# The opening of an attention and gated FFN kernel: crossed loads of values, another order of loads, and another order of all instructions up to the first split of h

## Chip, core and metric

The kernel runs on one core of a Trainium2 chip. The metric is the time of one execution on the device in microseconds (us). The kernel before takes 872.77 us, the median of three runs (871.47, 872.77, 873.49).

## What is computed

Attention over chunks of 64 positions, and a gated FFN over its result:

```python
# q, k, v: (8 batches, 8 heads, 576, 64), drawn as normal * 0.1, q and k times about 4
nc = S // chunk                               # 9 chunks of 64
scores = D ** -0.5 * matmul(q_c, k_c.transpose(0, 1, 2, 4, 3))
scores = scores - max(scores, axis=-1, keepdims=True)
attn = exp(scores)
attn = attn / (sum(attn, axis=-1, keepdims=True) + 1e-9)
x = matmul(attn, v_c)                         # to (4608 tokens, 512)
g = x @ w_gate                                # 512 -> 1536
h = g / (1 + exp(-g)) * (x @ w_val)
out = h @ w_out                               # 1536 -> 512
```

Inputs and outputs are float32.

## The kernel before

The 4608 tokens go in nine blocks of 512 (`N`), the 1536 inner columns in twelve parts of 128. A block's attention gives x turned, 512 features by 512 tokens, in four pieces of 128 features, one for each pair of heads. To keep precision, every factor of a product is split into an upper part in fp32r and a lower part, the rest; a product of a part (`Product`, `some`, L492) is three matmuls of 128x512 for each of the four pieces: upper by upper, upper by lower, lower by upper. For each part f a gate product (g) and a value product (v) are made, h = silu(g)\*v, h is split again, and `project` (L556 to L558) adds its products with w_out to the block's output. The weights come as 64-bit words and are joined to float32 by four steps (`scale`, `shift`, `below`, `join`, L87 to L97) and split by two more (`upper`, `lower`).

The change lies in the opening, where nothing is in memory yet and the attention of the first two blocks, a0 and a1, is done. Four head pairs make a block, two pairs make a `Couple` (class at L653). Its steps have one letter each, and they run in this order:

- S: scores of a pair (L304, 16 calls of 64x64, which the trace shows as 32 matmuls), on TensorE (PE).
- M: row maxima, on VectorE (DVE, L674). K: the maxima rounded (L678) and the rest of the rounding (L679), on DVE.
- B: two matmuls (L685) subtract the maxima from one of the couple's two banks of scores, on PE.
- E: exponentials of a bank, on ScalarE (ACT, L689). Z: their sums, DVE (L695). R: plus 1e-9 and the reciprocal, DVE (L458, L459).
- N: scores times reciprocals (L463), on DVE or on GpSimd (POOL), as L702 says: for the first couples of a0 and of a1 it is POOL.
- T: four transposes of a pair on PE (L468). C: their copy out by ACT (L708).
- X: values times probabilities of a couple (L482, 32 calls, 64 matmuls in the trace), on PE. U and L: split of the result into upper (ACT, L635) and lower part (DVE, L639).

A string (L730 to L736) is the order in which the program issues these steps, and the engines keep it, since PE, ACT and DVE are scheduled by hand. In a step such as M101 the first digit is the block, the second the pair (for S, T, C, U, L) or the couple, and the third, if any, the bank. `.8` is eight warm-up transposes of an identity (`keep_warm`, L58), whose results nobody reads. G0_12 and V0_12 are matmuls of a0's products with the first gate and value part: piece 1, third kind. Two letters are steps of weights (vs, vh, vb, vj, vu, vl: scale, shift, below, join, upper, lower of the value half of part 0; g of its gate half; w1 and w2 of parts 1 and 2). H0 is the silu of a0's first part, Q0 its product with the value. e0 and e1 are exchanges (L423): the values of a pair lie with its first head in partitions 0 to 63 and its second in 64 to 127, and X needs those of odd pairs with the halves swapped, so four ACT copies (a0) and four POOL copies (a1) of 64x512 make swapped ones (L425).

Loads are issued by SyncE (SP) in program order, L605 to L620, under a manual schedule for SP that ends with the opening. `load_v` (L420) brings the values of two pairs with one transfer of 512 KB; a pair's q and k are 512 KB, a `Half` of a weight part 512 KB, an `Up` part 1 MB.

After the string (L761 to L782) come a1's two products of part 0 (pg, pv), h1, the steps of w_out's first part (o), the split of h0 (`parts`), of w_out (`out_weights`), and `lag`, which keeps a projection back until the next one is due.

## Time and profile before

| | |
|---|---|
| runs (us) | 871.47, 872.77, 873.49; median 872.77 |
| profiled execution: span from the first to the last instruction | 870.3 us |
| runs' median less that span | 2.5 us |
| PE busy | 858.3 us, 99% of the span |
| weight loads (PEld) / DVE / ACT / POOL busy | 708.2 / 652.7 / 428.9 / 97.6 us |
| mean granted clock of PE | 0.999 |
| transfers | 217.51 MB, 250 GB/s in the mean |

The span is that of one profiled execution, which gives no other time of its own; what of a run lies around the span is read off the median. PE's busy time counts pipelined matmuls; weight loads (PEld) overlap them. A wait is written as the instruction that waited and, behind the arrow, what released it. Instructions of one line that follow each other stand in one row of the timeline.

### The profile page before, as it was taken

Reading aid. Unit: us, or ns where it says so; the run is one execution under the profiler, and the core shown is the slowest. Engines: PE = TensorE matmul, PEld = TensorE weight load, DVE = VectorE, ACT = ScalarE, POOL = GpSimd, SP = SyncE. Lnnn points to the kernel's source line nnn. Section 1 sums busy time; section 2 is a strip of 40 time slices with the busy share of each in tenths; the row PEclk is TensorE's granted clock in tenths of the full one; section 3 lists DMA queues with packets and bytes.
Section 4 is the critical chain, followed back from the end, with each engine's and each line's share of the span. In section 5 each row is a group of like instructions: output and inputs, shape, how many; then the busy total and the mean of one; then the engine's idle time right before and its main releaser. Section 6 shows DMA issues by size and latency. Waiting matters only on the chain.

```text
span 870.3 us, 14879 instructions
## 1 busy us (share of the span) xinstructions
PE 858.3 (99%) x5941; PEld 708.2 (81%) x5941; DVE 652.7 (75%) x923; ACT 428.9 (49%) x609; POOL 97.6 (11%) x86
## 2 busy tenths in 40 slices
PE   7999999999999999999999999999999999999997
...
GB/s 357 264 275 263 272 273 352 293 309 358 283 337 341 249 335 255 242 249 281 238 220 227 251 320 235 194 218 193 178 202 226 211 250 182 192 191 207 188 197 89
DMA packets 127221, 217.51 MB, mean 250 GB/s; under 512 B 57136, under 2 KB 88368, under 8 KB 117168
## 3 DMA queue, kind: packets, MB, share of 16 engines
...
## 4 chain that ended last, share of the span: by engine, by line
PE 88%; DVE 7%; DMA 2%; issue 1%; ACT 1%; SPq 0%; ACTq 0%; DVEq 0%
PE ps_a L880 24%; PE ps_gv L880 18%; PE ps_o L1229 14%; PE ps_gv L492 12%; PE ps_gv L1229 6%; PE ps_o L556 4%; PE ps_o L557 3%; PE ps_o L558 3%; PE ps_a L304 2%; PE ps_a L382 1%; DMA raw<-in_wgv 1%; DVE turned L369 1%; DMA factors<-t 1%; DVE v L884 1%; DVE rows L531 1%
## 5 line engine op out<-in xcount | busy, mean ns | idle before, releaser
L880 PE MATMUL ps_a<-x,factors 128*128 128x512 f32 x864 | 216.5, 391 | 0.5 <-DVE v L884 0.5
L880 PEld LDWEIGHTS ps_a<-x,factors 128*128 128x128 f32 x864 | 161.2, 188 | 36.8 <-DVE v L884 1.7
L880 PE MATMUL ps_gv<-x,factors 128*128 128x512 f32 x648 | 164.6, 389 | 1.0 <-DMA factors<-t 1.0
L880 PEld LDWEIGHTS ps_gv<-x,factors 128*128 128x128 f32 x648 | 121.5, 188 | 26.8 <-DMA factors<-t 1.4
L492 PE MATMUL ps_gv<-xh,w 128*128 128x512 f32 x320 | 97.9, 391 | 0.2 <-ACT xh L635 0.2
L369 DVE STREAM_TRANSPOSE turned<-s_sb 32x256 f32<-32x256 f32 x192 | 83.7, 436 | 2.7
L1229 PE MATMUL ps_o<-halves,sums 128*128 128x512 f32 (+1 forms) x324 | 72.5, 383 | 0.0
L492 PEld LDWEIGHTS ps_gv<-xh,w 128*128 128x128 f32 x320 | 59.8, 188 | 12.9 <-ACT xh L635 0.5
L1229 PEld LDWEIGHTS ps_o<-halves,sums 128*128 128x128 f32 x324 | 59.7, 188 | 12.0
L884 DVE TENSOR_TENSOR rows<-rows,ps_gv 128x512 f32<-128x512 f32 x36 | 24.7, 686 | 52.6 <-PE ps_gv L880 52.4
L531 DVE SCALAR_TENSOR_TENSOR rows<-v,rows 128x512 f32<-128x512 f32 x72 | 54.2, 752 | 12.8 <-ACT rows L1367 5.6
L1211 ACT CAST hh<-rows 128x512 fp32r<-128x512 f32 x36 | 22.4, 622 | 80.1 <-DVE rows L531 80.1
L492 PE MATMUL ps_gv<-xl,w 128*128 128x512 f32 x160 | 61.4, 393 | 0.0
L1229 PE MATMUL ps_o<-hh,left 128*128 128x512 f32 x216 | 58.4, 394 | 0.0
L556 PE MATMUL ps_o<-both,hh 128*128 128x512 f32 x144 | 56.4, 391 | 0.0
L557 PE MATMUL ps_o<-both,hh 128*128 128x512 f32 x144 | 56.0, 389 | 0.0
L558 PE MATMUL ps_o<-both,hh 128*128 128x512 f32 x144 | 56.0, 389 | 0.0
L1354 ACT ACTIVATE rows<-rows 128x512 f32<-128x512 f32 x36 | 22.8, 632 | 67.1 <-DVE rows L884 67.0
L1272 DVE TENSOR_TENSOR halves<-rows,halves 128x1024 fp32r<-128x1024 f32 x36 | 43.1, 1214 | 11.1 <-ACT halves L1268 11.1
L1229 PE MATMUL ps_gv<-halves,sums 128*128 128x512 f32 x216 | 50.4, 389 | 0.0
L1268 ACT CAST halves<-rows 128x1024 fp32r<-128x1024 f32 x36 | 37.2, 1053 | 21.4 <-DVE rows L1246 7.7
L1229 PEld LDWEIGHTS ps_gv<-halves,sums 128*128 128x128 f32 x216 | 40.5, 188 | 8.4
...
## 6 DMA issues: line engine op xcount, KB each, us to landing
...
```

The source lines that it names most:

```text
L369: nc.vector.transpose(out=self.turned[to:to + 32, p:p + 2, j, :, 32 * (i % 2):32 * (i % 2) + 32], in_=src[32 * i:32 * i + 32, :, o // 2, 3 ...
L492: nc.tensor.matmul(ps, w, x, start=first and (k, i) == which[0], stop=last and (k, i) == which[-1])
L531: nc.vector.scalar_tensor_tensor(out=h, in0=pv, scalar=2.0 ** -8, in1=h, op0=ALU.mult, op1=ALU.mult)
L556: nc.tensor.matmul(o, hl[:, ts], woh, start=f == a.steps[0], stop=False)
L557: nc.tensor.matmul(o, hh[:, ts], wol, start=False, stop=False)
L558: nc.tensor.matmul(o, hh[:, ts], woh, start=False, stop=f == a.steps[1])
L880: nc.tensor.matmul(ps, w[u][:, k], x[i][v][:, k], start=first and k == 0 and n == 0, stop=k == NK // 2 - 1 and n == 2, skip_group_check=True)
L884: nc.vector.tensor_tensor(out=t, in0=t, in1=ps, op=ALU.add)
L1229: nc.tensor.matmul(to, w[:, i, u], a[:, at], start=first and n == 0, stop=n == 2, skip_group_check=True)
L1268: nc.scalar.copy(out=t[:, 0], in_=src)
L1272: nc.vector.tensor_tensor(out=lo, in0=src, in1=hi.bitcast(F32), op=ALU.subtract)
L1354: nc.scalar.activation(h, h, AF.Silu, scale=2.0 ** -8)
```

## The change

Values of odd pairs are loaded swapped: `load_v` takes the first pair with one transfer of 128 partitions and the second with two of 64, each into the other half of the partitions, and the exchanges go. The loads stand in another order, and POOL is scheduled by hand in the opening as well. N is on POOL for both couples of a0 and the second of a1. The string is new; it now holds also a1's products (A gate, D value), the steps of w_out (o), h1 (H1), and the splits of h0 (hu, hl) and of w_out (ou, ol). The warm-ups before the loop become the string's first step.

```diff
--- before.py
+++ after.py
@@ -418,11 +418,10 @@
             return x[:, h * k:(h + 2 * y) * k].rearrange("p (i y k) -> p i y k", i=2, k=k)[:, :, 0:2 * T - 1:2]
 
         def load_v(self, p, t):
-            nc.sync.dma_start(out=t, in_=v[:, p:p + t.shape[1], self.b])
-
-        def exchange(self, t, to, copy=nc.gpsimd.tensor_copy):
+
+            nc.sync.dma_start(out=t[:, 0], in_=v[:, p, self.b])
             for h in range(2):
-                copy(out=to[h * C:(h + 1) * C], in_=t[(1 - h) * C:(2 - h) * C])
+                nc.sync.dma_start(out=t[h * C:(h + 1) * C, 1], in_=v[(1 - h) * C:(2 - h) * C, p + 1, self.b])
 
         def maxima(self, ps, m=None, tag="top"):
 
@@ -595,38 +594,31 @@
         nc.scalar.dma_start(out=waiting[f], in_=h)
 
     kept_h = []
-    loading = tc.manual_schedule(engines={mybir.EngineType.SP})
+    loading = tc.manual_schedule(engines={mybir.EngineType.SP, mybir.EngineType.Pool})
     loading.__enter__()
     a0, a1 = First(0), First(1)
     a1.places()
     a0.places()
     w, o = up[0], down[0]
-    q00 = a0.load_qk(0)
-    q01 = a0.load_qk(1)
-    wv = Half(w, 1)
-    q02 = a0.load_qk(2, 2, const, "w4")
     v0 = const.tile([P, NP, 2 * T, C], F32, name="v_t", tag="w3")
     v0 = [v0[:, p:p + 2] for p in (0, 2)]
+    q02 = a0.load_qk(2, 2, const, "w4")
+    q01 = a0.load_qk(1)
+    q00 = a0.load_qk(0)
+    q10 = a1.load_qk(0, 2, const, "w5")
+    wg = Half(w, 0)
+    q12 = a1.load_qk(2, 2, const, "w6")
+    wv = Half(w, 1)
+    a0.load_v(2, v0[1])
     a0.load_v(0, v0[0])
-    wg = Half(w, 0)
-    q10 = a1.load_qk(0, 2, const, "w5")
-    a0.load_v(2, v0[1])
-    q12 = a1.load_qk(2, 2, const, "w6")
     up[1].load()
     v1 = [ld.tile([P, 2, 2 * T, C], F32, name="v_t", tag="qk_t") for _ in range(2)]
+    a1.load_v(2, v1[1])
     a1.load_v(0, v1[0])
-    a1.load_v(2, v1[1])
     up[2].load()
     down[0].load()
     q0, q1 = [[q00, q01], [q02]], [[q10], [q12]]
-    values = []
-    for a, vs in ((a0, v0), (a1, v1)):
-        for c in range(2):
-            pool, tag = (ld, "v_t") if a is a0 else (wp, "wo")
-            odd = pool.tile([P, 2 * T, C], F32, name="v_t", tag=tag)
-            if a is a1:
-                a.exchange(vs[c][:, 1], odd)
-            values.append((vs[c][:, 0], odd))
+    values = [(t[:, 0], t[:, 1]) for t in v0 + v1]
 
     def x_of(a, p):
         return [x[:, p % 2] for x in a.x[p // 2]]
@@ -699,7 +691,7 @@
             self.a.inverse(self.z[:, :4 * T])
 
         def N(self, _):
-            self.a.scale(self.p, self.z[:, :4 * T], nc.gpsimd if (self.a.b, self.p) in ((0, 0), (1, 0)) else nc.vector)
+            self.a.scale(self.p, self.z[:, :4 * T], nc.gpsimd if (self.a.b, self.p) in ((0, 0), (0, 2), (1, 2)) else nc.vector)
 
         def T(self, q):
             self.a.turn_to(q, self.bank(1, [T, P])[q % 2])
@@ -724,29 +716,52 @@
             couples[a.b, c] = Couple(a, c, qs, values[2 * a.b + c], pools)
     products, h0 = {}, None
     steps = {"s": "scale", "b": "below", "h": "shift", "j": "join", "u": "upper", "l": "lower"}
-    weights = {"g": wg, "v": wv, "w1": up[1], "w2": up[2]}
-
+    weights = {"g": wg, "v": wv, "w1": up[1], "w2": up[2], "o": o}
+
+
+    class FirstPart:
+        def upper(self):
+            self.hh, self.hl = both_parts()
+            nc.scalar.copy(out=self.hh, in_=h0)
+
+        def lower(self):
+            nc.vector.tensor_tensor(out=self.hl, in0=h0, in1=self.hh.bitcast(F32), op=ALU.subtract)
+
+    class FirstOut:
+        def upper(self):
+            both = wp.tile([P, 2, DM], F32R, name="both", tag="wo")
+            out_now[0], self.both = both, (both[:, 0], both[:, 1])
+            nc.scalar.copy(out=self.both[0], in_=wo_raw[0])
+
+        def lower(self):
+            nc.vector.tensor_tensor(out=self.both[1], in0=wo_raw[0], in1=self.both[0].bitcast(F32), op=ALU.subtract)
+            t = store.tile([P, 2, 2, DM], F32, name="o0")
+            kept_o[0], kept_o[1], two_o[0] = t[:, 0], t[:, 1], t
+
+    first_part, first_out = FirstPart(), FirstOut()
 
     opening = """
-        S00 S01 M001 M000 vs K00 vh vb .8 B001 B000 vj E001 Z001 E000 e0 .3 S02 Z000 S03 R00 N00 M010 M011 gs
-        .10 T01 K01 gh gb C01 B011 B010 E011 T00 gj Z011 E010 Z010 R01 C00 S10 gu S11 X00 vu M101 U01 .3 V0_12
-        M100 U00 K10 G0_12 B101 e1 E101 N01 L01 B100 T02 E100 gl T03 C03 vl G0_10 S13 S12 C02 L00 M111 M110 X01
-        V0_01 w1s K11 G0_11 G0_01 U02 G0_02 U03 Z100 Z101 B111 B110 V0_21 V0_32 V0_10 w1b L02 R10 G0_22 G0_21
-        E111 V0_02 Z111 V0_22 V0_11 L03 G0_00 E110 G0_32 G0_20 G0_31 N10 V0_00 Z110 G0_30 V0_31 V0_20 V0_30 R11
-        N11 T10 T11 T13 Y0 w2s H0 w1h Q0 C10 w1j C11 T12 C12 C13 X10 U11 X11 L11 U10 U12 U13 L10 L13 w1u L12
+        .37 S03 S02 S01 M011 M010 .3 S00 K01 M001 B011 B010 M000 E011 E010 K00 .2 S10 Z011 S11 Z010 B001 M101
+        B000 E001 M100 E000 R01 gs K10 Z000 N01 .11 B100 B101 Z001 E100 S12 gb R00 S13 Z100 E101 N00 T03 M111
+        T02 C03 M110 vs Z101 C02 .6 T01 K11 T00 vb R10 B110 gh C00 B111 N10 E110 X01 E111 C01 gj T11 U03 vh
+        T10 gu X00 vj U02 gl vu G0_32 Z110 G0_22 U01 G0_21 G0_31 U00 Z111 V0_32 V0_12 C11 V0_22 vl G0_12 C10
+        V0_02 R11 G0_02 w1s V0_11 V0_01 L01 N11 X10 L00 Y0 L03 G0_10 V0_10 G0_01 L02 V0_31 G0_30 U10 T13 U11
+        T12 L10 G0_11 G0_00 C12 L11 G0_20 V0_21 C13 V0_30 w1h V0_20 H0 V0_00 X11 w1b Q0 A_12 A_01 U13 w1j A_10
+        D_02 U12 A_02 A_32 os D_12 L13 A_31 D_22 A_22 L12 A_00 w1u D_30 D_32 oh A_11 D_01 ob A_30 w1l D_31
+        A_21 A_20 D_10 D_21 H1 oj D_20 D_00 hu D_11 ou hl w2s ol
     """
-    keep_warm(15)
+    of = {"G": (a0, 0, 0), "V": (a0, 0, 1), "A": (a1, 0, 0), "D": (a1, 0, 1)}
     for do in opening.split():
         if do[0] == ".":
             keep_warm(int(do[1:]))
-        elif do[0] in "gvw":
+        elif do[0] in "hou" and do in ("hu", "hl", "ou", "ol"):
+            getattr(first_part if do[0] == "h" else first_out, steps[do[1]])()
+        elif do[0] in "gvwo":
             getattr(weights[do[:-1]], steps[do[-1]])()
-        elif do[0] in "GV":
+        elif do[0] in "GVAD":
             if do[0] not in products:
-                products[do[0]] = Product(a0, 0, "GV".index(do[0]))
-            products[do[0]].add((int(do[3]), int(do[4])))
-        elif do[0] == "e":
-            a0.exchange(v0[int(do[1])][:, 1], values[int(do[1])][1], nc.scalar.copy)
+                products[do[0]] = Product(*of[do[0]])
+            products[do[0]].add((int(do[-2]), int(do[-1])))
         elif do == "Y0":
             h0 = hp.tile([P, N], F32, name="h")
             nc.scalar.activation(h0[:, :1], ident[:, :1], AF.Silu)
@@ -754,6 +769,8 @@
             nc.scalar.activation(h0, products["G"].ps, AF.Silu, scale=2.0 ** -8)
         elif do == "Q0":
             times(h0, products["V"].ps)
+        elif do == "H1":
+            h1 = silu(products["A"].ps)
         else:
             b, i = int(do[1]), int(do[2])
             pairs = do[0] in "STCUL"
@@ -762,22 +779,10 @@
     up[3].load()
     down[1].load()
     down[2].load()
-    w = up[1]
-    pg, pv = Product(a1, 0, 0), Product(a1, 0, 1)
-    pg.add((0, 1), (1, 1), (0, 2), (1, 2), (2, 1), (3, 1), (2, 2), (3, 2))
-    pv.add((0, 1), (1, 1), (0, 2), (1, 2))
-    pg.add((0, 0), (1, 0), (3, 0), (2, 0))
-    o.scale()
-    o.below()
-    h1 = silu(pg.ps)
-    pv.add((0, 0), (1, 0), (2, 1), (3, 1), (2, 2), (3, 2), (2, 0), (3, 0))
-    pv1 = pv.ps
-    w.lower()
+    pv1 = products["D"].ps
     save_w(1)
-    o.shift()
-    o.join()
-    p0 = parts(a0, 0, h0)
-    wo_f = out_weights(0)
+    p0 = a0, 0, first_part.hh, first_part.hl
+    wo_f = first_out.both
     lag(p0, wo_f)
     down[1].scale()
 
```

The start of PE: matmuls by line, operation, result and factors, shape and count. unread is a warm-up, ps_a<-qk_t scores (S), ps_a<-tops,minus the maxima's subtraction (B), ps_a<-ident,s_sb a pair's transposes (T). Before:

```order
L58 MATMUL unread<-ident 128x128 x15
L304 MATMUL ps_a<-qk_t 64x64 x32
L58 MATMUL unread<-ident 128x128 x8
L685 MATMUL ps_a<-tops,minus 128x512 x4
L58 MATMUL unread<-ident 128x128 x3
L304 MATMUL ps_a<-qk_t 64x64 x32
L58 MATMUL unread<-ident 128x128 x10
L468 MATMUL ps_a<-ident,s_sb 128x128 x4
```

After:

```order
L58 MATMUL unread<-ident 128x128 x37
L304 MATMUL ps_a<-qk_t 64x64 x48
L58 MATMUL unread<-ident 128x128 x3
L304 MATMUL ps_a<-qk_t 64x64 x16
L677 MATMUL ps_a<-tops,minus 128x512 x4
L58 MATMUL unread<-ident 128x128 x2
L304 MATMUL ps_a<-qk_t 64x64 x32
L677 MATMUL ps_a<-tops,minus 128x512 x4
L58 MATMUL unread<-ident 128x128 x11
L677 MATMUL ps_a<-tops,minus 128x512 x4
L304 MATMUL ps_a<-qk_t 64x64 x32
L467 MATMUL ps_a<-ident,s_sb 128x128 x8
```

Of the first warm-ups there are 37 instead of 15; three pairs' scores follow them in one piece, and the fourth's stand behind three more warm-ups.

DVE where it ends the sums of the first couples (names carry buffer numbers: z are sums, both the maxima of a couple, tops their rounded parts). Before (z_221 is a0's first couple, both_268 and tops_289 its second):

```order
L695 TENSOR_REDUCE z_221<-s_sb_100 128x2x4 x2
L458 TENSOR_SCALAR z_221<-z_221 128x16
L459 RECIPROCAL z_221<-z_221 128x16
L674 TENSOR_REDUCE both_268<-ps_a_230 128x8
L674 TENSOR_REDUCE both_268<-ps_a_231 128x8
L678 CAST tops_289<-both_268 128x16
L679 TENSOR_TENSOR tops_290<-both_268,tops_289 128x16
```

After (z_297 is a0's second couple, z_332 its first, both_318 and tops_328 are a1's first couple):

```order
L666 TENSOR_REDUCE both_318<-ps_a_280 128x8
L666 TENSOR_REDUCE both_318<-ps_a_279 128x8
L457 TENSOR_SCALAR z_297<-z_297 128x16
L458 RECIPROCAL z_297<-z_297 128x16
L670 CAST tops_328<-both_318 128x16
L671 TENSOR_TENSOR tops_329<-both_318,tops_328 128x16
L687 TENSOR_REDUCE z_332<-s_sb_100 128x2x4 x2
L457 TENSOR_SCALAR z_332<-z_332 128x16
L458 RECIPROCAL z_332<-z_332 128x16
```

Before, the maxima stood between the reciprocal and K; now K of a1's first couple stands directly behind the first reciprocal, which releases the first scaling on POOL, and the sums, the addition and the reciprocal of a0's first couple behind it.

POOL in the same stretch. Before:

```order
masks.py:199 AFFINE_SELECT ident_88<-ident_88 128x128
L463 TENSOR_TENSOR s_sb_100<-s_sb_100,z_221 128x1024
L425 COPY v_t_140<-v_t_130 64x512 x2
L425 COPY v_t_143<-v_t_131 64x512 x2
L463 TENSOR_TENSOR s_sb_101<-s_sb_101,z_509 128x1024
L195 TENSOR_TENSOR th_2666<-w_2586 128x512 x2
```

After:

```order
masks.py:199 AFFINE_SELECT ident_88<-ident_88 128x128
L462 TENSOR_TENSOR s_sb_100<-s_sb_100,z_297 128x1024
L462 TENSOR_TENSOR s_sb_100<-s_sb_100,z_332 128x1024
L462 TENSOR_TENSOR s_sb_101<-s_sb_101,z_533 128x1024
L195 TENSOR_TENSOR th_2682<-w_2602 128x512 x2
L155 TENSOR_TENSOR th_2682<-th_2682 128x512
```

The four copies are gone, and two scalings of a0 follow each other.

SP from its first load on. Before:

```order
L276 DMA qk_t<-in_qk 128x1024 x2
L227 DMA raw<-in_wgv 128x512
L276 DMA qk_t<-in_qk 128x2x1024
L421 DMA v_t<-in_v 128x2x512
L227 DMA raw<-in_wgv 128x512
L276 DMA qk_t<-in_qk 128x2x1024
L421 DMA v_t<-in_v 128x2x512
L276 DMA qk_t<-in_qk 128x2x1024
L116 DMA raw<-in_wgv 128x1024
L421 DMA v_t<-in_v 128x2x512 x2
L116 DMA raw<-in_wgv 128x1024
L252 DMA raw<-in_wo 128x2x512
```

After:

```order
L276 DMA qk_t<-in_qk 128x2x1024
L276 DMA qk_t<-in_qk 128x1024 x2
L276 DMA qk_t<-in_qk 128x2x1024
L227 DMA raw<-in_wgv 128x512
L276 DMA qk_t<-in_qk 128x2x1024
L227 DMA raw<-in_wgv 128x512
L422 DMA v_t<-in_v 128x512
L424 DMA v_t<-in_v 64x512 x2
L422 DMA v_t<-in_v 128x512
L424 DMA v_t<-in_v 64x512 x2
L116 DMA raw<-in_wgv 128x1024
```

The 1 MB of q02 is first, q of a1 stands ahead of the weights and of all v, and each load of v is three transfers.

## Rows read from the trace of the kernel before

**Rows 1.** The page of the profiled execution: its span, and busy time, share of the span and number of instructions of each engine.

```profile
span 870.3 us, 14879 instructions
PE 858.3 (99%) x5941; PEld 708.2 (81%) x5941; DVE 652.7 (75%) x923; ACT 428.9 (49%) x609; POOL 97.6 (11%) x86
```

**Rows 2.** The waits of PE over the whole span: tile and line that waited, what released it, total us, how often, and the longest.

```profile
PE ps_a L304 <- DMA qk_t<-in_qk: 1.6, 2, 0.8
PE unread L58 <- POOL ident masks.py:199: 1.4, 1, 1.4
PE ps_gv L880 <- DMA factors<-t: 1.0, 1, 1.0
PE ps_a L304 <- DVE xl L639: 0.8, 1, 0.8
PE ps_a L468 <- POOL s_sb L463: 0.7, 1, 0.7
PE ps_a L685 <- DVE tops L678: 0.7, 1, 0.7
PE ps_a L880 <- DVE v L884: 0.5, 2, 0.3
...
```

**Rows 3.** Two windows of the span: stretch, its length, busy us (and instructions) of PE, PEld, DVE, ACT and POOL, the granted clock, the share of the DMA engines and GB/s.

```profile
0.00:46.70 46.70, 40.95 (x671) 34.18 (x672) 35.12 (x62) 33.31 (x52) 6.94 (x12) 1.00 0.83 318
46.70:870.30 823.60, 817.32 (x5271) 674.07 (x5269) 617.55 (x862) 395.58 (x558) 90.63 (x74) 1.00 0.74 246
```

**Rows 4.** The timeline of PE and its weight loads (PEld) in the opening, and the first two products of h with w_out that follow it: start, length, engine, line, operation, count, and in brackets the idle time before and what ended it.

```profile
1.36 3.06 PEld L58 LDWEIGHTS unread<-ident 128*128 128x128 f32 x15 [1.36 <-POOL ident masks.py:199]
...
4.75 1.46 PEld L304 LDWEIGHTS ps_a<-qk_t 64*64 64x64 f32 x64 [0.33 <-DMA qk_t<-in_qk]
...
10.26 1.02 PEld L304 LDWEIGHTS ps_a<-qk_t 64*64 64x64 f32 x64 [1.01 <-DMA qk_t<-in_qk]
...
11.35 1.07 PEld L58 LDWEIGHTS unread<-ident 128*128 128x128 f32 x10
...
33.30 2.24 PEld L482 LDWEIGHTS ps_a<-pT,v_t 64*64 64x64 f32 x128 [0.17 <-issue]
...
35.66 2.62 PEld L492 LDWEIGHTS ps_gv<-xh,w 128*128 128x128 f32 x12
...
46.70 0.39 PE L556 MATMUL ps_o<-both,hh 128*128 128x512 f32 x1
...
47.15 0.39 PE L558 MATMUL ps_o<-both,hh 128*128 128x512 f32 x1
```

**Rows 5.** The timeline of DVE: the first maxima (L674) and their rounding (L678, L679), in the columns of rows 4.

```profile
6.42 1.29 DVE L674 TENSOR_REDUCE both<-ps_a 128x8 f32<-128x512 f32 x2 [6.42 <-PE ps_a L304]
...
7.74 0.17 DVE L678 CAST tops<-both 128x16 fp32r<-128x16 f32 x1
7.95 0.17 DVE L679 TENSOR_TENSOR tops<-both,tops 128x16 fp32r<-128x16 f32 x1
```

**Rows 6.** The timeline of DVE and POOL around the four POOL instructions of the opening (two scalings, L463, and four copies, L425), in the columns of rows 4.

```profile
11.01 0.25 DVE L459 RECIPROCAL z<-z 128x16 f32<-128x16 f32 x1
...
11.41 1.90 POOL L463 TENSOR_TENSOR s_sb<-s_sb,z 128x1024 f32<-128x1024 f32 x1 [10.11 <-DVE z L459]
...
12.80 0.55 DVE L678 CAST tops<-both 128x16 fp32r<-128x16 f32 x1
...
23.75 2.58 POOL L425 COPY v_t<-v_t 64x512 f32<-64x512 f32 x4 [10.43 <-DMA v_t<-in_v]
...
25.74 0.61 DVE L679 TENSOR_TENSOR tops<-both,tops 128x16 fp32r<-128x16 f32 x1
...
28.25 0.26 DVE L459 RECIPROCAL z<-z 128x16 f32<-128x16 f32 x1
28.42 0.63 DVE L695 TENSOR_REDUCE z<-s_sb 128x8 f32<-128x512 f32 x1
28.68 1.90 POOL L463 TENSOR_TENSOR s_sb<-s_sb,z 128x1024 f32<-128x1024 f32 x1 [2.36 <-DVE z L459]
...
30.27 0.34 DVE L458 TENSOR_SCALAR z<-z 128x16 f32<-128x16 f32 x1
```

**Rows 7.** The second load of the kernel, q01, by itself: nanoseconds of its issue (least, median, most), when it was issued, and us from issue to landing.

```profile
L276 SPq DMA_DIRECT2D qk_t<-in_qk x1: 421/421/421, 1.2 to 1.2; - x1
...
DMA to landing us min/median/max: 4.4/4.4/4.4
```

**Rows 8.** The timeline of instructions that waited for a load (columns as in rows 4): of w_v's half (L87 at 7.61), of v of a0's first couple (L425 on ACT), of w_g's half (L87 at 13.69), and of q of a1's first couple (L304).

```profile
7.61 0.66 ACT L87 ACTIVATE t<-raw 128x512 f32<-128x512 f32 x1 [5.27 <-DMA raw<-in_wgv]
...
11.81 1.25 ACT L425 COPY v_t<-v_t 64x512 f32<-64x512 f32 x2 [1.96 <-DMA v_t<-in_v]
...
13.69 0.66 ACT L87 ACTIVATE t<-raw 128x512 f32<-128x512 f32 x1 [0.63 <-DMA raw<-in_wgv]
...
16.17 1.02 PEld L304 LDWEIGHTS ps_a<-qk_t 64*64 64x64 f32 x64 [1.08 <-DMA qk_t<-in_qk]
```

**Rows 9.** Three loads of v for a later block, two of them of 64 of the 128 partitions (L1027) and one of all (L1023): nanoseconds of an issue (least, median, most), when they were issued, and us from issue to landing.

```profile
L1027 SPq DMA_DIRECT2D v_t<-in_v x2: 472/530/587, 192.1 to 192.6; - x2
L1023 SPq DMA_DIRECT2D v_t<-in_v x1: 535/535/535, 191.5 to 191.5; - x1
...
DMA to landing us min/median/max: 7.0/7.1/7.2
```

## The prediction

> **What bounds the kernel now.** I read the page's busy line first: TensorE (PE) is busy 99% of the span, so only what PE waits for, or does needlessly, can give time back [rows 1]. Then the waits of PE: 7.4 us in all, of which only the two L880 rows (1.5 us) lie behind the opening; the rest, loads of q and k, the mask of ones, DVE's and POOL's steps of the softmax, stand in the first 47 us [rows 2]. The windows say the same: in 0 to 46.70 us PE is busy 40.95, in the 823.6 us behind it 817.3 [rows 3]. 46.70 is where the first product of h with w_out (L556) starts [rows 4]. Ahead of it both kernels make the scores, the transposes and X of eight pairs, 16 matmuls with the maxima and 72 products; after it they have the same PE work in the same order. So I forecast where that L556 comes to lie; what it moves, the end moves. The profiled span is 870.3; the runs' median of 872.77 stands 2.5 above it, and I take that 2.5 as unchanged.
>
> **What PE needs without waits.** Prices from [rows 4], by weight-load starts. Two head pairs of scores: 10.26 to 11.35, 1.09; four times, 4.4. A 128x128 transpose: 10 in 1.07, 0.11; 32 of them, 3.5. X of two couples: 33.30 to 35.66, 2.36; twice, 4.7. A 128x512 product: 46.70 to 47.15 for two, 0.225; 72 products and 16 with the maxima, 16.2 and 3.6. Sum 32.4.
> Before: PE starts at 1.36, its 15 warm-ups take 3.06 (at half pace, 0.22 each), the first scores 0.44 longer than later ones (1.46 against 1.02), 24 more warm-ups 2.6: 1.36 + 3.06 + 0.44 + 2.6 + 32.4 = 39.9. So 6.8 of the 46.70 are waits and gaps.
> After: 37 warm-ups stand first. PE's pace tells of its clock: from 1.36 on it runs at half of the later pace, the lower of the two levels, 1.2 of 2.4 GHz, though the granted clock reads 1.00 over the whole stretch [rows 3]. PE did 3.4 us of transposes, then scores, and 0.44 lost at half pace puts the rise 0.88 us into these, near 5.6. If it comes at 5.6 again, 19 warm-ups fill 1.36 to 5.6 and 18 at 0.11 take 2.0, to 7.6; the other 22 take 2.4. 7.6 + 2.4 + 32.4 = 42.4. The change can give back 4.3 at most, less the waits that its own order has.
>
> **The waits of the new order**, walked with the rows' durations. The loads: what landed is read from what waited for it. 1.0 MB had landed at 1.2 + 4.4 = 5.6, 1.5 at 7.6, 2.5 at 10.2, 3.0 at 11.8, 3.5 at 13.7, 4.5 at 16.1, 7.5 at 23.7 [rows 4, 6, 7, 8], nearly 2.5 us per MB. By the new order's bytes q02 lands at 5.6, q01 7.6, q00 8.9, q10 11.8, wg 13.7, q12 16.1, wv 17.4, v of a0 18.6 and 19.8, v of a1 23.6 and 24.85.
> - S03 S02 S01 from 7.6, three warm-ups, S00: to 10.2. The first two M (1.29 for two [rows 5]) can start when S02 is through, at 8.9, and end at 10.3; with CAST (0.17) the first B starts at 10.5: 0.3 of wait.
> - S10 wants q10 (3.0 MB, 11.8): 0.15.
> - B100, behind 11 warm-ups, wants M and K of a1's first couple: 0.15.
> - T01, behind six, wants N00. POOL does N01 first, and while POOL works DVE's small steps stand: CAST at 12.80 took 0.55 instead of 0.17 and ended with POOL's scaling (11.41 + 1.90), TENSOR_TENSOR at 25.74 took 0.61, TENSOR_SCALAR at 30.27 0.34 [rows 6]. R01's reciprocal ends about 15.1, N01 takes POOL 15.3 to 17.2, R00's TENSOR_SCALAR (due 16.65) is held to 17.2, its reciprocal ends 17.5, N00 takes POOL to 19.55, and PE, free at 18.85, waits 0.75.
> - X10 wants a copy of T from ACT: 0.1. From there I find none up to L556; h's and w_out's splits end 4 us before it.
> Sum 1.45. Changes from one kind of instruction to another add 0.25, and the same walk through the kernel before ends 0.2 short of its trace. 42.4 + 1.45 + 0.25 + 0.2 = 44.3: **L556 comes 2.35 us earlier.**
>
> **Part by part.** The 15 to 37 and 24 to 22 warm-ups: PE would wait for q02 there anyway; 22 more of them cost at most 2.4. What is late next is T01, then the loads.
> The exchange: two pairs of ACT copies and four POOL copies (2.58, [rows 6]) go. They stood beside PE's work. What they cost is their hold on DVE at 25.74: 0.44 there, contained in the 6.8. N on POOL three times instead of two: 1.90 each, beside products, except where T01 waits (counted) and except the port (below).
> The crossed loads: 12 DMAs for 4, SP issues each in about 0.5 [rows 9], and 8 more fit in the time in which it waits for landings. Half-partition loads of 128 KB: no such row in the opening. By bytes 0.31 each. At 192 us two of them and one full load are issued at 191.5, 192.1 and 192.6 and land 7.0 to 7.2 later, so about 0.5 apart [rows 9]: at 0.5, eight come 1.6 later in all, at 0.59 2.2 later. v of a1's first couple, needed by X10 at 27.4, then lands at 26.5 to 27.1. I take 0.5, cost nothing; a gain is excluded, the bytes being the same. The cover is 0.3 to 2.5 us; gone, each later us costs PE one.
> w_v's half lands at 17.4 instead of 7.6 and feeds its first product at 25.7: 8 us for its six short steps on ACT and DVE (the first takes 0.66 [rows 8]), hidden. SP's few swaps near 190 us move loads that no PE wait names [rows 2]: nothing.
>
> The Trainium skill has a rule on the hold of POOL on DVE, in "SBUF — State Buffer", section "SBUF: two separate sides": the two engines share a pair of ports, and whichever starts first keeps the other out for the whole instruction. The trace agrees (0.55 and 0.61 where 0.17 is usual). By this rule the order of two starts decides, which is the first rival.
>
> **Rivals.**
> 1. *POOL takes the port first (0.25).* K10's second step, a TENSOR_TENSOR on DVE, comes 0.1 behind R01's reciprocal, as does N01. In the trace the instruction after a reciprocal started 0.09 before its end (28.25 + 0.26, then 28.42); CAST to TENSOR_TENSOR is 0.21 [rows 5], so DVE gets there 0.12 after it. POOL started 0.15 and 0.17 after (11.26 to 11.41, 28.51 to 28.68 [rows 6]). DVE leads by 0.03 to 0.05. That can fall the other way: TENSOR_TENSOR at 25.74 had begun 0.02 behind POOL's last copy and was held. Then K10 ends at 17.2 instead of 15.4, B100 waits 1.8 more, T01 0.4 less: L556 at 45.75, **gain 0.95, 871.8**.
> 2. *The clock rises with the scores, not with the time (0.10).* In the trace 3.4 us of transposes stood ahead and the pace doubled only 0.88 into the scores [rows 4]. If transposes alone don't raise it, 37 cost 8.1 (to 9.5), and the rise comes at 10.4: each later us of rise costs half a us, 4.8 make 2.4. **No gain, 872.8.** Against it: a level once granted stayed through the 10 transposes at 11.35, and the rise may simply have been due.
> The Trainium skill's page "TensorE: Matmul & The Clock Gate", section "Part 4: PE-mode transpose", says that transposes don't count as PE activity for the clock. By it this rival holds; whether the warm-ups here are transposes in that sense no run shows, and the 10 at 11.35 neither fit nor refute it.
> 3. *Slower: the half-partition loads of v (0.05).* If each takes 1.1 to 1.2 instead of 0.5 (twice the largest spacing), v of a1's first couple lands at 31 to 32; X10 waits from 27.4 on, and the products that could stand in lie behind it on PE. It decides from a landing later than about 27.5, that is 0.63 per load. L556 at 48.5 to 49.3: **about 2.2 slower, 875.0**. For it: no crossed load was seen while the queue was this full. Against: 0.5 at 192 us.
> The rest (0.05): the loads come otherwise than by bytes, for instance q10 one us later than 11.8 (S10 and all behind it wait 0.55 to 0.8).
>
> **How the numbers follow.** Likeliest, 0.55: 872.77 − 2.35 = 870.4, alone 869.6 to 871.3 (gaps of 0.5 not in the walk, runs that spread 2 us). The measurement can tell about 0.2%, 1.75 us, from no change: 871.0. Of the likeliest case about 0.43 lies below that, of the first rival 0.05, of the rest 0.02: faster 0.50. Above 874.5 lie rival 3 and a little of 2 and the rest: 0.07. Same: 0.43. The range 869.0 to 873.3 takes in the likeliest case, rival 1 and most of rival 2; what is left out is rival 3 and the tails.
>
> **What would show it.** In the profile after: the first scores (S03) start at 7.6 and take 1.0 per two pairs (if 2.0, rival 2). B100 starts near 15.2 and K10's TENSOR_TENSOR takes 0.17; if it takes 1.9, rival 1. T01 waits 0.7 for POOL near 19.6. X10 starts near 27.5; a DMA wait of PE on v there is rival 3. L556 starts near 44.3, and between it and the end lies the same 823.6. I am wrong if L556 comes 2.3 earlier and the span doesn't, or if PE waits in a place not listed.

## The result, and the profile after

The changed kernel takes 881.25 us (median of four runs, 880.15 to 883.26); the kernel before took 873.13 in the four runs beside it (871.47 to 874.77). The ratio is 1.0099 [1.0083, 1.0116]: 8.1 us slower, where I had forecast 2.4 faster. The profiled execution took 880.21. The page, as in [rows 1], and one line of its part on DMA queues (packets, MB, share of 16 engines):

```profile
span 878.4 us, 14925 instructions
PE 863.0 (98%) x5961; PEld 712.6 (81%) x5961; DVE 650.6 (74%) x922; ACT 426.7 (49%) x605; POOL 97.6 (11%) x83
...
q8 instruction: 47, 0.77, 0.4%
```

The windows, cut where the first product with w_out starts (L555 now), as in [rows 3]:

```profile
0.00:51.89 51.89, 45.17 (x692) 38.31 (x693) 31.76 (x61) 30.98 (x48) 6.42 (x9) 0.97 0.79 291
51.89:878.40 826.51, 817.83 (x5271) 674.32 (x5269) 618.86 (x863) 395.67 (x558) 91.22 (x74) 1.00 0.73 245
```

That product comes 5.2 us later than before and 7.6 later than forecast; the rest, which I took as unchanged, is 2.9 longer. So there are two losses to find, one on each side of it. PE's waits, as in [rows 2]:

```profile
PE ps_a L481 <- issue: 3.1, 2, 2.8
PE ps_a L304 <- issue: 1.8, 1, 1.8
PE ps_o L555 <- DVE hh L63: 1.5, 1, 1.5
PE unread L58 <- POOL ident masks.py:199: 1.4, 1, 1.4
PE ps_gv L885 <- DMA factors<-t: 1.3, 1, 1.3
PE ps_a L885 <- DVE v L889: 1.1, 2, 0.8
PE ps_a L467 <- POOL s_sb L462: 0.3, 1, 0.3
```

The first two are of a kind that [rows 2] do not have: "issue", a wait for nothing that the profile shows. In the timeline of weight loads, as in [rows 4], they stand in the middle of steps:

```profile
1.36 6.40 PEld L58 LDWEIGHTS unread<-ident 128*128 128x128 f32 x37 [1.36 <-POOL ident masks.py:199]
7.93 1.49 PEld L304 LDWEIGHTS ps_a<-qk_t 64*64 64x64 f32 x96 [0.17 <-issue]
...
12.05 0.83 PEld L304 LDWEIGHTS ps_a<-qk_t 64*64 64x64 f32 x49 [0.17 <-issue]
14.82 0.32 PEld L304 LDWEIGHTS ps_a<-qk_t 64*64 64x64 f32 x15 [1.94 <-issue]
15.21 0.73 PEld L677 LDWEIGHTS ps_a<-tops,minus 128*128 128x128 f32 x4
...
23.37 0.19 PEld L481 LDWEIGHTS ps_a<-pT,v_t 64*64 64x64 f32 x3 [0.33 <-ACT pT L700]
24.00 1.13 PEld L481 LDWEIGHTS ps_a<-pT,v_t 64*64 64x64 f32 x61 [0.44 <-issue]
25.20 0.86 PEld L467 LDWEIGHTS ps_a<-ident,s_sb 128*128 128x128 f32 x8
26.23 0.95 PEld L481 LDWEIGHTS ps_a<-pT,v_t 64*64 64x64 f32 x57 [0.17 <-issue]
30.08 0.26 PEld L481 LDWEIGHTS ps_a<-pT,v_t 64*64 64x64 f32 x7 [2.91 <-issue]
30.46 4.03 PEld L491 LDWEIGHTS ps_gv<-xh,w 128*128 128x128 f32 x12
```

S11 stops after 49 of its 64 loads, X01 after 3, X00 after 57. Nothing new is wanted there: the calls of one step read the same tiles. Counted over all rows of the view, the stops come after 223 loads, 127 further on, and 126 further on. The page's line of instruction packets gives the same number: 47 packets in 0.77 MB are 16 KB each, and 5961 matmuls with a weight load each over 47 are 127. (That q8 carries PE's code is read from this count; the page has a second queue of instructions, q14, with 22 packets in 0.18 MB, which are of another size.) So the theory, **F**: PE's instructions come from memory in blocks of 16 KB, about 127 matmuls; PE stops where a block ends and the next is not there.

### The profile page after: what moved, and what is told of

It is laid out like the page before. It is cut to its first block, busy times and chain, and to the rows that moved or that the text cites. A ratio compares the mean times of both kernels' runs of the same rounds, so it can differ in the third digit from the quotient of the medians.

```text
span 878.4 us, 14925 instructions
## 1 busy us (share of the span) xinstructions
PE 863.0 (98%) x5961; PEld 712.6 (81%) x5961; DVE 650.6 (74%) x922; ACT 426.7 (49%) x605; POOL 97.6 (11%) x83
## 4 chain that ended last, share of the span: by engine, by line
PE 89%; DVE 6%; DMA 2%; issue 1%; ACT 1%; POOL 0%; ACTq 0%; SPq 0%; DVEq 0%; POOLq 0%
PE ps_a L885 24%; PE ps_gv L885 18%; PE ps_o L1234 13%; PE ps_gv L491 12%; PE ps_gv L1234 6%; PE ps_o L555 3%; PE ps_o L557 3%; PE ps_o L556 3%; PE ps_a L304 2%; PE ps_a L382 1%; DVE turned L369 1%; DMA factors<-t 1%; PE ps_a L481 1%; PE unread L58 1%; DVE v L889 1%
## 5 line engine op out<-in xcount | busy, mean ns | idle before, releaser
L885 PEld LDWEIGHTS ps_gv<-x,factors 128*128 128x128 f32 x648 | 121.5, 188 | 27.1 <-DMA factors<-t 1.7
L555 PE MATMUL ps_o<-both,hh 128*128 128x512 f32 x144 | 56.5, 392 | 1.5 <-DVE hh L63 1.5
L557 PE MATMUL ps_o<-both,hh 128*128 128x512 f32 x144 | 56.0, 389 | 0.0
L1273 ACT CAST halves<-rows 128x1024 fp32r<-128x1024 f32 x36 | 37.2, 1053 | 21.5 <-DVE rows L1251 7.7
```

The source lines that it names most:

```text
L555: nc.tensor.matmul(o, hl[:, ts], woh, start=f == a.steps[0], stop=False)
L557: nc.tensor.matmul(o, hh[:, ts], woh, start=False, stop=f == a.steps[1])
L885: nc.tensor.matmul(ps, w[u][:, k], x[i][v][:, k], start=first and k == 0 and n == 0, stop=k == NK // 2 - 1 and n == 2, skip_group_check=True)
L1273: nc.scalar.copy(out=t[:, 0], in_=src)
```

## The experiments

F's rivals stand in the expectations. These count every weight load, also some that the timeline leaves out, and so say 225, 355 and 485 for 223, 350 and 476; some of their times of the first product are by its weight load, 0.22 earlier than its matmul, which the table gives. "Behind" is the span less that time. Edits are to the changed kernel where nothing else is said.

| kernel | median us | ratio to before | first product | behind | "issue" waits in the opening |
|---|---|---|---|---|---|
| before | 872.5 to 873.1 | | 46.70 | 823.6 | none above 0.2 |
| after | 881.25 | 1.0099 [1.0083, 1.0116] | 51.89 | 826.5 | 1.8, 0.3, 2.8 |
| warm15 | 874.54 | 1.0022 [1.0009, 1.0036] | 46.60 | 829.0 | 2.2 in two |
| warm18 | 872.31 | 0.9995 [0.9983, 1.0007] | 47.08 | 824.3 | 1.9 |
| oneload | 879.48 | 1.0083 [1.0059, 1.0107] | 49.61 | 825.1 | 1.2, 2.7 |
| fullparts | 876.90 | 1.0051 [1.0033, 1.0069] | 49.64 | 825.3 | 1.9, 2.2 |
| crossed_only | 874.70 | 1.0026 [1.0014, 1.0039] | 47.98 | 823.4 | none |
| merged18 | 874.09 | 1.0016 [1.0001, 1.0031] | 47.31 | 824.4 | 2.3 in two |
| x00late | 878.55 | 1.0062 [1.0047, 1.0077] | 52.25 | 824.1 | 2.1, 1.1 |
| light | 876.54 | 1.0047 [1.0028, 1.0066] | 48.97 | 825.4 | 1.6; 1.6 in three |
| wide7 | 875.75 | 1.0037 [1.0023, 1.0051] | 46.15 | 825.9 | 1.0, 0.6 |
| after_fix | 878.69 | 1.0075 [1.0059, 1.0092] | 53.20 | 823.2 | 2.1, 2.5 |
| wide_fix | 873.40 | 1.0009 [0.9999, 1.0018] | 48.22 | 824.1 | 1.4, 1.0 in two |
| swapped_in_memory | 870.75 | 0.9978 [0.9967, 0.9990] | 44.77 | 823.6 | 1.2 |

### Do the stops follow the count of instructions?

**warm15**: 22 warm-ups fewer, so that the same count lies elsewhere in the program.

```diff
-        .37 S03 S02 S01 M011 M010 .3 S00 ...
+        .15 S03 S02 S01 M011 M010 .3 S00 ...
```

> The changed kernel with 15 first warm-ups instead of 37, nothing else. Theory F (PE's own instructions come from memory in blocks of about 127 matmuls with their weight loads; the next block is asked for when PE enters the present one, and comes 6 to 9 us later while the loads run): 22 instructions fewer let PE enter each block later in the program, so the stops at 14.8 and 30.1 us (1.8 and 2.8 us) go or shrink to under 0.7 us together, the clock does not fall at 30 us, and the first product with w_out (L555) starts at 45 to 46 instead of 51.9; time 873 to 875. Theory D (PE stops for values that arrive late through the half-partition loads, or for other data): the loads are the same, the stops stay at their place in the program, L555 stays at 51 to 52; 880 to 882. Theory C (the clock alone): no stop goes, the first scores run at half pace for longer; 881 to 883.

Weight loads of warm15:

```profile
13.11 0.86 PEld L58 LDWEIGHTS unread<-ident 128*128 128x128 f32 x8 [0.19 <-issue]
...
20.39 0.44 PEld L481 LDWEIGHTS ps_a<-pT,v_t 64*64 64x64 f32 x24 [0.33 <-ACT pT L700]
22.55 0.67 PEld L481 LDWEIGHTS ps_a<-pT,v_t 64*64 64x64 f32 x40 [1.72 <-issue]
```

The first block now ends among warm-ups, after 3 of 11, and costs 0.19; the second ends after 24 of X01's 64 and costs 1.7; the third costs 0.7. The counts are 223, 349 and 475: the stops went with the count and left the places. The first product is at 46.60, 5.3 earlier. But 829.0 lie behind it, so the kernel is still no faster than before. (The profiled run, 877.41, stands 2.9 above the median; a fall of the clock behind the first product, 3.4 us at the lower level, is in it.)

**x00late**: the third block's end stays in X00, but X00 comes behind five products (the expectation says six).

```diff
-        T10 gu X00 vj U02 gl vu G0_32 Z110 G0_22 U01 G0_21 G0_31 U00 Z111 V0_32 V0_12 ...
+        T10 gu vj U02 gl vu G0_32 Z110 G0_22 G0_21 G0_31 V0_32 X00 U01 U00 Z111 V0_12 ...
```

> The changed kernel with X of a0's first couple behind six products of its second couple instead of ahead of them. F: the stop stands at the same count of matmuls (near the 476th), so X00 stops 6 matmuls earlier in itself; the products fill 1.4 us of the wait, the stop falls from 2.8 to 1.3 to 1.8 us, the clock may stay up; the stop of 1.8 in S11 stays. L555 at 48.5 to 50.5. The order of SP's later loads near 196 us happens to be that of the kernel before here: if that order cost the 1.8 us of PE's wait there, this wait is 0.2 again. Together 876 to 879. D: X00 waits for data until 30 us as before, the products being done earlier: stop of 1.4 too, but at X00's first matmul.

```profile
28.64 0.89 PEld L481 LDWEIGHTS ps_a<-pT,v_t 64*64 64x64 f32 x53 [0.37 <-DMA v_t<-in_v]
30.79 0.31 PEld L481 LDWEIGHTS ps_a<-pT,v_t 64*64 64x64 f32 x11 [1.25 <-issue]
```

X00 goes on after 53 of 64, behind a stop of 1.25 instead of 2.91: a block that PE takes longer to use up hides more. The first product was a miss: 52.25, not earlier, since PE's clock fell at 15.9, behind the first stop, and again at 33.0.

### Is it the loads that make a block late?

In the table of DMA queues of after, from 24.0, when PE enters the third block, to 27.5 nothing but loads runs:

```profile
q1 hardware_dynamic: 277, 1.20, 105.7%
```

and the block's packet comes in 27.5 to 28.7, with PE at a stand since 27.2:

```profile
q1 hardware_dynamic: 112, 0.46, 94.3%
q8 instruction: 1, 0.02, 5.5%
```

**light** takes loads away there: a1 uses a0's values, and the weights of part 2 and of w_out's first part are loaded later, behind the write of part 0's.

```diff
-    v1 = [ld.tile([P, 2, 2 * T, C], F32, name="v_t", tag="qk_t") for _ in range(2)]
-    a1.load_v(2, v1[1])
-    a1.load_v(0, v1[0])
-    up[2].load()
-    down[0].load()
+    v1 = v0
```

> The changed kernel without the loads of a1's v (a1 uses a0's values, so a1's part of the output is not that of the reference) and with the loads of the third weight part and of w_out's first behind the write of part 0's weights (near 29 us). The count of instructions is unchanged; from 24 us on hardly a load is under way. F with the queue (a block of instructions waits behind the loads in the DMA engines): the stop behind the 225th weight load stays (1.5 to 2.2), the one behind the 485th falls from 2.8 to under 0.7, the clock does not fall; L555 at 47 to 48.5; 876 to 877.5. F with a fixed delay of some 6 us for a block: the stop of 2.8 stays; 880 to 882.

In light the same table for 23.75 (entry of the block) to 26.2 has the packet alone:

```profile
q8 instruction: 1, 0.02, 3.4%
```

and the stop after the same 57 loads shrinks from 2.91 to 0.71:

```profile
25.98 0.95 PEld L481 LDWEIGHTS ps_a<-pT,v_t 64*64 64x64 f32 x57 [0.17 <-issue]
27.64 0.20 PEld L481 LDWEIGHTS ps_a<-pT,v_t 64*64 64x64 f32 x7 [0.71 <-issue]
```

The first stop, at 12.8, where the loads are still the same, stays (1.6). The next end of a block, 126 loads further on, in X10 at 37.1, now costs 0.7, where after passes it without a stop: the loads that were put off fill the queue there (99.2% from 30.0 to 34.8, when its packet comes). In the trace the packet stands at 24.97 in light, 1.2 behind the entry of the block, and PE goes on 2.7 behind it. In after it stands at 27.6, 3.6 behind the entry, and PE goes on 2.5 behind it; for the block before, entered at 14.82 under loads that fill the queue as much (103.9% from 15.0 to 21.4), it stands at 21.5, 6.7 behind, and PE goes on at 24.00, again 2.5. So what loads lengthen is the time until the packet moves, and that loads do it is shown by taking them away; a fixed delay of 6 us, the expectation's rival, is out.

The clock is the second part of the loss. These windows of after are the third block with its stop, the time behind it, and the next (columns as in [rows 3]):

```profile
24.00:30.08 6.08, 3.27 (x126) 2.94 (x126) 4.23 (x9) 2.78 (x6) 0.64 (x1) 1.00 1.04 370
30.08:33.60 3.52, 3.52 (x15) 2.74 (x15) 2.40 (x4) 3.02 (x5) 1.27 (x1) 0.52 0.76 320
33.60:37.20 3.60, 3.60 (x75) 2.78 (x74) 0.61 (x2) 2.65 (x5) 0.00 (x0) 1.00 0.03 11
```

After the pause of 2.8 the granted clock is at its lower level, 0.52 of 2.4 GHz, for 3.5 us. The twelve products there take 4.4, from 30.46 to 34.86; twelve took 2.66 in before (from 35.66 in [rows 4] to the next product at 38.32), so 1.7 is lost. In light, behind 0.6 of pause, the clock stays at 1.00. The length of a pause alone does not say whether the clock falls: behind stops of 1.9 it fell to 0.50 in warm18 (from 23.0 on) and in fullparts (from 15.3 on), each time for 3.4 us, and behind 1.8 in after and 2.2 in fullparts it did not.

**wide7** keeps PE as long at work with fewer instructions: 7 warm-ups and 13 matmuls of 128x512 in place of 37 warm-ups.

```diff
-        .37 S03 S02 S01 M011 ...
+        .7 ,13 S03 S02 S01 M011 ...
...
+    def keep_wide(n):
+        ps = ps_gv.tile([P, N], F32, name="unread", tag="ps_gv")
+        for _ in range(n):
+            nc.tensor.matmul(ps, minus, minus[:, :1].broadcast_to([P, N]), start=True, stop=True)
```

> The changed kernel with 7 narrow first warm-ups and 13 matmuls of 128x512 in place of the 37: PE is as busy and starts its scores near 7.3 (7.9 in the changed kernel, 5.6 with 15), but 17 instruction pairs fewer stand ahead. F (it is the count of instructions): stops again behind the 225th and the 485th weight load, each a little shorter, 1 to 1.8 and 0.5 to 1.5 us; L555 at 48 to 50; 877 to 880. P (the 15 warm-ups help because the scores start 2 us earlier): stops at the places of the changed kernel, in S11 and X00 behind 49 and 57 matmuls, L555 at 51 to 52; 880 to 882.

The first product came at 46.15, better than expected: the blocks end at 224, 350 and 476 as before, but elsewhere in the program, and cost 1.2, 0.8 and 0.35 by the weight loads; no clock fall. That the scores started at 6.56 instead of the expected 7.3 is chance: in the profiled execution the pace of the warm-ups doubled at 4.3, in that of wide_fix at 7.2, behind the same 20 warm-ups. The stops followed the count; how much of the 5.7 us came from the count and how much from the earlier start, this run does not show.

### What do the crossed loads cost by themselves?

**oneload** brings a couple's values with one transfer, **fullparts** keeps three transfers but gives each all 128 partitions; in both the odd pairs' values are not crossed.

```diff
+            nc.sync.dma_start(out=t, in_=v[:, p:p + 2, self.b])                    # oneload
...
+                nc.sync.dma_start(out=t[:, 1, part], in_=v[:, p + 1, self.b, part])   # fullparts
```

> The changed kernel with the values of two pairs loaded by one transfer, as before, and no exchange, so that the values of odd pairs are not crossed and the attention of the first two blocks uses the wrong halves for them: bytes as before, 4 transfers instead of 12. F: the stops stand at the same counts of matmuls, L555 within 0.7 of 51.9; 880 to 882. D: v comes up to 2 us earlier, the stop of 2.8 us in X00 goes and with it the fall of the clock; L555 near 47.5, 876 to 877.

> The changed kernel with each half-partition load of 64x512 replaced by one of 128x256 (same bytes, same number of transfers, values not crossed, so the attention of the first two blocks uses wrong halves for odd pairs). If it is the number of small transfers that slows the loads: the third weight part lands near 30 as in the changed kernel (29.7); 880 to 882. If it is the 64 partitions: it lands near 27.3 as with one transfer per couple, 878.5 to 880.

Both are 2.3 earlier at the first product, and both keep stops of 1.2 to 2.7 at the counts of after: the crossed loads make the stops longer (4.9 in sum against 3.9 and 4.1) but are not their cause. F had the place of the stops right and the time wrong: it expected the first product of oneload within 0.7 of 51.9. What the crossed loads cost is read off the last load in the queue, part 2's weights. In after (issue, then us to landing):

```profile
L116 SPq DMA_DIRECT2D raw<-in_wgv x1: 1086/1086/1086, 21.8 to 21.8; - x1
...
DMA to landing us min/median/max: 7.9/7.9/7.9
```

and in fullparts:

```profile
L116 SPq DMA_DIRECT2D raw<-in_wgv x1: 438/438/438, 20.0 to 20.0; - x1
...
DMA to landing us min/median/max: 7.3/7.3/7.3
```

29.7 against 27.3. Eight half-partition loads cost 2.4, or 0.30 each beyond their bytes' 0.31, in the mean and in this order: the weights of part 1, behind four of them, are already 2.0 late (24.1 against 22.1), and other orders pay more, warm18 2.9 in all (30.3 against 27.4 in swapped_in_memory below) and crossed_only 3.7 (31.0 against 27.3 in before). In oneload it is 27.3 too, so the number of transfers does not matter. The profiled spans of the two agree (874.7 and 874.9); why oneload's median is 2.6 higher stays open.

**crossed_only** is the kernel before with the crossed loads and without the copies.

```diff
-            nc.sync.dma_start(out=t, in_=v[:, p:p + t.shape[1], self.b])
+            nc.sync.dma_start(out=t[:, 0], in_=v[:, p, self.b])
+                nc.sync.dma_start(out=t[h * C:(h + 1) * C, 1], in_=v[(1 - h) * C:(2 - h) * C, p + 1, self.b])
...
-            a0.exchange(v0[int(do[1])][:, 1], values[int(do[1])][1], nc.scalar.copy)
```

> The kernel before with the crossed loads of v (12 transfers for 4) and without the ACT and POOL copies; its order of steps, loads and warm-ups unchanged. F: PE has 39 warm-ups and products between its scores as before, no block is late; without POOL's copies on DVE's way L556 starts 0.3 to 0.5 earlier than 46.7; 872.3 to 873 (ratio 0.999 to 1.000). D: v late by 1.6 to 2 us and more where it is the crossed loads that stop PE: L556 at 48 to 50, 875 to 877.

A miss: slower, not faster, though no block is late, as F had it. q10, which stands behind two half-partition loads in that order, lands at 18.2 instead of 16.1, S10 waits 2.5 for it where [rows 8] have 1.08, and the first product comes 1.3 later. So crossed loads can also cost by the data that stand behind them.

**warm18** takes 18 warm-ups, and **merged18** also puts a0's values into three transfers instead of six.

```diff
+        .18 S03 S02 S01 M011 M010 .3 S00 ...                                       # both
...
+            nc.sync.dma_start(out=t[:, 0:n:2], in_=v[:, p:p + n:2, self.b])        # merged18
+                nc.sync.dma_start(out=t[h * C:(h + 1) * C, 1:n:2], in_=v[(1 - h) * C:(2 - h) * C, p + 1:p + n:2, self.b])
```

> The changed kernel with 18 first warm-ups; PE's opening as with 15, but the scheduler now puts SP's loads near 196 us in the order of the kernel before (the load of h_in again ahead of two loads of v and two stores). Theory F with S (the swapped order of SP near 196 us makes PE wait for h's split there): L555 at 46 to 47, the wait of PE for the split of h (L63) near 198 us falls from 2.4 to 0.3 or less and the clock does not fall there; 3 to 4 us less than with 15 warm-ups: 870.5 to 871.8. If that wait does not hang on SP's order: it stays at 1.5 to 2.4, 873.5 to 875.

> As the one with 18 first warm-ups, and v of a0's two couples loaded by three transfers (one of 512 KB, two half-partition ones of 256 KB) instead of six. If the half-partition loads are slow because small transfers leave too little in flight (SP has at most eight outstanding): the loads behind them land 0.5 to 1 us earlier, PE's blocks of instructions too, L555 at 45.3 to 46.2, 869.8 to 871.3. If they are slow because of their 64 partitions: as with six, 870.5 to 871.8.

warm18 gained 2.2 on warm15, less than expected, and by the profiles behind the first product (824.3 against 829.0), where it has no swap of SP's loads (below) and no wait for L63; its second block's stop is 1.9, behind which the clock fell. merged18's last load lands at 30.2, as warm18's (30.3): again it is the partitions, not the number of transfers. Its time of 874.09 is above both ranges that were expected: PE also waits 0.9 there for the values of X01.

### Where do the 2.9 us behind the first product go?

Most of it is in waits. In the list of after, L555 waits 1.5 for L63, the split of h that has come back from memory; before has no such wait. The waits for factors and v are 2.4 in all, where [rows 2] have 1.5. The load of that h, in after and, in the second fence, in before:

```profile
L986 SPq DMA_DIRECT2D h_in<-h x1: 452/452/452, 195.8 to 195.8; - x1
...
DMA to landing us min/median/max: 6.2/6.2/6.2
```

```profile
L981 SPq DMA_DIRECT2D h_in<-h x1: 382/382/382, 189.5 to 189.5; - x1
...
DMA to landing us min/median/max: 4.2/4.2/4.2
```

Reckoned from the first product it is issued some 1.0 later (at 195.75 in after, 189.54 in before), behind two loads of v and two stores where before has one of each, and takes 2.0 longer. ACT, DVE and PE of after wait for it:

```profile
202.04 1.14 ACT L62 CAST hh<-h_in 128x512 fp32r<-128x512 f32 x2 [4.84 <-PE ps_o L557]
...
203.44 0.50 PE L555 MATMUL ps_o<-both,hh 128*128 128x512 f32 x1 [1.51 <-DVE hh L63]
```

The bracket of the ACT row names PE: its L557 ended at 201.93, and h landed at 201.95, so the trace cannot tell which of the two held ACT; the next run can. The order of SP there is the scheduler's, and it is one of the "few swaps near 190". **after_fix** ties the loads of v behind that of h.

```diff
+        with tc.issue_after(fetched[1]):
+            load_later()
```

> The changed kernel, only that the four transfers of v for the third block, which SP issues near 195 us, are held behind the second load of h_in there, so that SP's order near 196 us is again that of the kernel before but for one place. S (that order makes PE wait for h's split): the opening as in the changed kernel, L555 at 51.2 to 52.6; PE's wait of 1.5 us for L63 near 203 us gone; 879 to 880. If the wait has another cause: it stays, 880.5 to 882.

The wait is gone, those for factors and v are 1.5 again, and 823.2 lie behind the first product, as before's 823.6: 3.3 less than in after. The span is only 2.0 shorter, since in the opening the clock fell twice (at 15.9 and 29.6) and the first product came 1.3 later. Over all versions it is the same: with a swapped order (after, warm15, oneload, fullparts, light, wide7) 825.1 to 829.0 lie behind the first product, with before's order (warm18, merged18, x00late, the two fixes, swapped_in_memory) 823.2 to 824.4. In warm15 the wait for L63 is 2.4, and the clock fell behind it.

**wide_fix** joins the fix with wide warm-ups in three places.

```diff
-        .37 S03 S02 S01 ...
+        .7 ,13 S03 S02 S01 ...
...
-        ... N01 .11 B100 B101 ...
+        ... N01 ,5 B100 B101 ...
...
-        ... C02 .6 T01 K11 ...
+        ... C02 ,3 T01 K11 ...
```

> All warm-ups but the first 7 and the five behind S01 and K00 made of wide matmuls (13 for 30, 5 for 11, 3 for 6: 26 instruction pairs fewer than in the changed kernel), and v of the third block held behind the second load of h_in. F: stops behind the 225th, 355th and 485th weight load of under 1.3, 0.7 and 0.5 us; L561 at 45 to 46.5. With S the wait near 197 us is gone too: 870 to 872.5. If only the starting time of the scores counts: as with 13 wide ones before, L561 at 45.9, and 873.5 to 875.5 if the order of SP is not at fault.

A miss in the opening: 48.22. The pace of the warm-ups doubled only at 7.2, so the scores started at 7.94, and the first stop was 1.4. The time is no different from before's.

### A version that is faster than both

If blocks are late because of loads, and crossed loads lengthen the queue, then the values should arrive crossed without half-partition loads: **swapped_in_memory** lays the input out with the halves of odd pairs exchanged for the first two blocks, loads a couple with one transfer, and takes 18 warm-ups.

```diff
+            nc.sync.dma_start(out=t, in_=v[:, p:p + 2, self.b])
...
+        .18 S03 S02 S01 M011 M010 .3 S00 ...
...
+    v[:, 1::2, :2] = np.concatenate([v[C:, 1::2, :2], v[:C, 1::2, :2]])
```

> The changed kernel with 18 first warm-ups (and so SP's order near 196 us as in the kernel before), and with the values of odd pairs of the first two blocks laid out with their halves swapped in the array that the kernel is given (as q, k, v are already laid out turned), so that one full transfer per couple brings them crossed: no half-partition loads, no copies. F and the price of half-partition loads: loads land 2.4 us earlier than with 18 warm-ups alone (the third weight part at 27.3 instead of 30.3), the stop of 2.0 us behind the 355th weight load shrinks to under 1, L555 at 44.8 to 46.0 instead of 46.9; 870.3 to 871.7, faster than both. If the stop does not follow the loads: as with 18 warm-ups alone, 871.8 to 873.

870.75 us, 0.9978 [0.9967, 0.9990] of before: 0.2% faster. The span, and PE's waits:

```profile
span 868.4 us, 14875 instructions
```

```profile
PE ps_a L304 <- DMA qk_t<-in_qk: 1.4, 3, 0.7
...
PE ps_a L479 <- issue: 1.2, 1, 1.2
```

The first product lies at 44.77. That this is near the 44.3 forecast for the change itself is chance: it has 19 warm-ups fewer, waits 1.4 for q in three places where the forecast had 0.15 in one, and stops for 1.2 at one late block, which was expected under 1. Part 2's weights land at 27.4, as expected; the gain on warm18 (872.31) is in the opening, where the profiled execution of warm18 also has the fall of the clock.

## Why the prediction was wrong

- **"The waits of the new order", "Sum 1.45"**, is the step that failed. The walk asked what data each step waits for, and not whether PE has its instructions; it has no wait in S11, X01 and X00, where PE stood for want of code. By PE's idle times the three ends of blocks cost 4.9. By the starts of weight loads, the prediction's own measure, they cost 5.8: S10 with S11 takes 3.16 (12.05 to 15.21), X01 1.83 (23.37 to 25.20) and X00 4.23 (26.23 to 30.46), where its prices are 1.09, 1.18 and 1.18. The clock that fell behind the third stop cost 1.7. The scores started 0.3 late (7.93 for 7.6), since the clock rose near 6.2 instead of 5.6: the warm-ups start 0.21 apart up to 6.1 and 0.11 apart from 6.3 on. Together that is 7.8 of the 7.6 by which the first product was late; what else differs, T01's shorter wait above all, cancels the 0.2. The prediction had named the sign itself: "if PE waits in a place not listed".
- **"22 more of them cost at most 2.4"**: with 15 the first product comes 5.3 earlier. The scores start 2.3 earlier (5.61 against 7.93), as I had reckoned; but the ends of the blocks move with them, which saves 2.7 of stops (by PE's idle times) and 1.7 of the clock fall, and waits for q and for ACT take 1.4 back.
- **The half-partition loads, "I take 0.5, cost nothing"**: the size, 0.61 in the mean of after, lay just inside the bound of 0.63 from which I had rival 3 decide (in warm18 and crossed_only it was 0.67 and 0.77), and v of a1's first couple landed at 27.5, later than my 26.5 to 27.1. PE waits for no v in after, so rival 3's mechanism did not occur. What the loads hold back is the instruction blocks, which the "cover" of 0.3 to 2.5 did not count.
- **"SP's few swaps near 190 us ... nothing"** is the second step that failed: 2.9 here, and 3.3 came back with after_fix. That no wait in [rows 2] named these loads only said that they were in time before; how much later they might be, I did not ask.
- **Right, with some luck**: POOL's port. DVE got there first, by 0.02, where 0.03 to 0.05 was forecast, as the DVE and POOL rows of after show:

```profile
16.74 0.25 DVE L458 RECIPROCAL z<-z 128x16 f32<-128x16 f32 x1
...
17.13 0.18 DVE L671 TENSOR_TENSOR tops<-both,tops 128x16 fp32r<-128x16 f32 x1
17.15 1.92 POOL L462 TENSOR_TENSOR s_sb<-s_sb,z 128x1024 f32<-128x1024 f32 x1 [15.85 <-ACT s_sb L681]
```

 So rival 1 did not occur, and T01's wait is there, 0.3 where I gave 0.75. Rival 2 is out: 37 warm-ups took 6.40, less than 37 at half pace (8.1), and the first 96 score loads took 1.49 at full pace. The clock rose while PE had done nothing but transposes.

The trace of before could have shown the danger. Counted in the same way, it enters its blocks at 10.27 (in the row at 10.26 of [rows 4]), 16.77 (in the row at 16.17 of [rows 8]), 23.15 and 30.15, in these rows:

```profile
22.85 0.96 PEld L304 LDWEIGHTS ps_a<-qk_t 64*64 64x64 f32 x59 [0.95 <-DVE xl L639]
...
30.15 0.19 PEld L492 LDWEIGHTS ps_gv<-xh,w 128*128 128x128 f32 x1
```

So a block there lasts 6.5, 6.4 and 7.0 us, waits for data and products among its short matmuls. Its packets stand at 11.64, 19.91 and 26.50, 1.4, 3.1 and 3.4 behind the entries; with the 2.5 that PE takes from a packet to going on, an estimate from after, the next block is there after 3.9, 5.6 and 5.9, in time by 0.8 and 1.1 for the last two. Two of these ends lie in the middle of scores, and nothing shows. In after, PE is through its blocks in 4.1 (8.76, in the row at 7.93, to 12.88), 8.7 (14.82 to 23.56) and 3.2 (24.00 to 27.18), and goes on after 6.1, 9.2 and 6.1. What the change did is to put scores and X, 64 short matmuls each, so close together that a block is used up sooner than the next one comes.

The Trainium skill's "Runtime: NRT & Kernel Launch", section "Instruction fetch mechanics", says that instructions come in blocks of 16 KiB, the next being fetched while the present one runs, and that crossing is mostly hidden. The runs agree on the blocks (127 matmuls apart); that it is mostly hidden holds for before, and not here, where a crossing cost up to 2.8 us.

What stays open: by what rule a packet of code gets its turn among the loads (1.2, 3.6 and 6.7 us behind the entry of a block), and when the clock rises or falls, which came out differently in runs of nearly the same work.
